# Fewer TensorE instructions for q and z, and other partitions for the gathered rows

## The chip, the cores and the metric

The kernel runs on one core of one Trainium2 chip. Its time is the device time of one execution in microseconds (us); lower is better. The core has TensorE (matmuls, "PE" in the profile, its weight loads "PEld"), VectorE ("DVE"), ScalarE ("ACT"), GpSimd ("POOL"), SyncE ("SP"), whose queue issues nearly all loads here, and 16 DMA engines that move the bytes.

## What is computed

One token of a decoder layer goes through an attention over a cache and through a gated MLP, and both results are added to the input. Cut to what matters, with D = 576, 32 query heads and 16 key heads of 128, a window W of 4096 positions, and F = 4608, Fh = 2304:

```python
xn = layernorm(x)
q = (xn @ wq).reshape(32, 128)
k, v = last W positions of the caches, each key head for two query heads
o = softmax(q @ k.T * 128 ** -0.5) @ v
z = gelu(xn @ w_in)                       # 4608 values
z1, z2 = z[:Fh], layernorm(z[Fh:])
g = w_sp * z2 + b_sp                      # one position: w_sp and b_sp are numbers
out = x + o.reshape(4096) @ wo + (z1 * g) @ w_out
```

All inputs and the output are bf16. The keys and values of the window are 16 MB each; with the four weight matrices about 51 MB have to be read for one token.

## The kernel before, in words

**Loads.** All large loads are issued by SyncE in one order: wq, K0, K1, w_in, K2, V0, K3, V1, V2, V3, then the ends (w_out, wo in five pieces). K and V come in four groups of four heads, each a tile of 128 partitions by 32768 bytes. There are four large buffers (a, b, c, d); a load waits until the work that reads its buffer's last content is done (lines 105 to 120).

**w_out and its gathered rows.** Row f of w_out belongs to partition f // 18, place f % 18. Of the 18 rows of a partition, 15 (NM) come with the load at line 117. The last three (NX) of each partition are 3456 bytes in one piece, and come through two indirect loads that GpSimd issues (load_ext, line 303), each for 128 partitions with an index for each of them. In the first, the partitions in SPARED have the index FAR, which is out of bounds, so nothing is moved for them. In the second, the partitions in GIVEN take the rows of the spared partitions, and all others are FAR. So 32 partitions' rows are loaded to other partitions. The matching values of the MLP are moved to the same partitions by a matmul with the 0/1 matrix `move` (line 546), into hx. The indices are built on GpSimd as a diagonal matrix (`both`, lines 269 to 284), turned into a column on TensorE (`pick`, lines 286 to 288) and cast by VectorE after the first key transposes (rows_to_take, line 290).

**q.** 36 matmuls make q in PSUM (qps), spread over partitions 0, 1, 32, 33, and so on (line 236). It is copied four times into q_rep, two copies by VectorE, two by ScalarE (lines 243 to 247), so that 16 matmuls can turn it into columns that stand in all four blocks of 32 partitions (line 253). Sixteen VectorE operations then write Qb, the weights for the scores, each with a mask (mask4) that leaves one block and zeros the rest (line 264).

**Attention.** For each group and each half of the window, VectorE transposes the keys in blocks of 32 (keys, line 321), and TensorE makes the scores with Qb (line 328). Softmax (sm_a, sm_b) and the products with V (pv, line 401) follow group by group; each group's result ends in Y (y_copy, line 434).

**z.** For each of 9 slices of w_in, z_mms runs eight matmuls of 288 columns: two halves of 9 places (ZT), each for four blocks of partitions (line 443). z_exp turns both halves with two transposes of VectorE (line 451), takes the two useful columns and starts the gelu.

**The order** of everything on each engine is written out by hand at the end (from line 501), and each engine runs its instructions in that order. The last piece is a row of matmuls with one column of weights each (out_mms, line 560): 15 places of hv with w_out, 32 of Y with wo, and the gathered rows with hv and hx.

Of the kernel before, what the change touches and what calls it, by code (L numbers as in the profile page):

```python
# [8 lines left out]
FP32 = mybir.dt.float32  # L9
BF16 = mybir.dt.bfloat16  # L10
# [3 lines left out]
AXX = mybir.AxisListType.X  # L14
# [3 lines left out]
HKV = 16  # L18
# [9 lines left out]
NR = 98  # L28
NF = FH // 128
# [3 lines left out]
NM = NF - NX  # L33
PAIRS = NF // NX
FAR = 4096
SPARED = ((20, 8), (52, 8), (84, 6), (90, 2), (116, 4), (120, 4))
GIVEN = (60, 68, 76, 0, 92, 8)
EPS = 1e-5
SCALE = DH ** -0.5
GELU_C = 0.7978845608028654  # L40
NS = 9
ZT = NF // 2


@with_exitstack
def kernel(
# [14 lines left out]
    nc = tc.nc  # L61
    P = nc.NUM_PARTITIONS
# [4 lines left out]
    const = ctx.enter_context(tc.tile_pool(name="const", bufs=1))  # L67
# [5 lines left out]
    more = ctx.enter_context(tc.tile_pool(name="more", bufs=1))  # L73
    ps_s = ctx.enter_context(tc.tile_pool(name="ps_s", bufs=1, space=bass.MemoryType.PSUM))
    ps_o = ctx.enter_context(tc.tile_pool(name="ps_o", bufs=1, space=bass.MemoryType.PSUM))
    ps_m = ctx.enter_context(tc.tile_pool(name="ps_m", bufs=1, space=bass.MemoryType.PSUM))
    ps_a = ctx.enter_context(tc.tile_pool(name="ps_a", bufs=1, space=bass.MemoryType.PSUM))
    ps_b = ctx.enter_context(tc.tile_pool(name="ps_b", bufs=1, space=bass.MemoryType.PSUM))
# [52 lines left out]
    ident = const.tile([P, P], BF16, name="ident")  # L131
    make_identity(nc, ident[:])
    ones_f = const.tile([P, P], FP32, name="ones_f")
# [10 lines left out]
    nc.vector.memset(qps[:], 0.0)  # L144
    mask = const.tile([P, 2], FP32, name="mask")
    nc.vector.reduce_sum(mask[:], ident[:].rearrange("p (r h) -> p h r", h=2), axis=AXX)
    mask4 = const.tile([P, 4], FP32, name="mask4")
    nc.vector.reduce_sum(mask4[:], ident[:].rearrange("p (a x) -> p a x", a=4), axis=AXX)

    cm = const.tile([P, 2, 2], FP32, name="cm")  # L150
    idc = ident[:].rearrange("p (q u y e) -> p u q y e", q=4, u=2, e=2)
    for e in range(2):
# [5 lines left out]
                            axis=mybir.AxisListType.XY)  # L158
# [17 lines left out]
    for n in range(2):  # L176
        t = ps_s.tile([P, 2, 512], FP32, name=f"S{n}")
# [17 lines left out]
    for j in range(NS):  # L195
        nc.tensor.matmul(ps_x[:, j:j + 1], lhsT=xtw[:, j].rearrange("p m h -> p (m h)"), rhs=ones_b[:, 0:1],  # L196
                         start=True, stop=True)
# [28 lines left out]
    move = more.tile([P, P], BF16, name="move")  # L226
    nc.vector.memset(move[:], 0.0)
    XZ = more.tile([P, NS, 32], BF16, name="XZ")
# [5 lines left out]
    for s, wv in wq_sb:  # L234
        for g in range(4):
            nc.tensor.matmul(  # L236
                qps[32 * g:32 * g + 2, :], lhsT=XT[:, s, :], rhs=wv[:, 512 * g:512 * (g + 1)],
                start=(s == 0), stop=(s == NS - 1), tile_position=(0, 32 * g),
            )

    q_rep = const.tile([P, 8, 2, 4, 32], BF16, name="q_rep")
    qsv = qps[:].rearrange("p (m d e) -> p m e d", e=2, d=32)
    for a in range(4):
        if a % 2:
            nc.scalar.copy(q_rep[:, :, :, a, :], qsv)  # L245
        else:
            nc.vector.tensor_copy(q_rep[:, :, :, a, :], qsv)  # L247

    qps2 = ps_m.tile([P, 4, 4, 8], FP32, name="qps2", tag="m")
    idq = ident[:].rearrange("p (g x) -> p x g", g=4)[0:NR, 0:2, :]  # L250
    for k in range(4):
        for be in range(4):
            nc.tensor.matmul(
                qps2[:, k, be, :].rearrange("p (r g) -> p r g", r=2),
                lhsT=q_rep[0:NR, 2 * k + be // 2, be % 2].rearrange("p a d -> p (a d)"),
                rhs=idq, start=True, stop=True)

    Qb = const.tile([P, HKV, 4, 4, 2], BF16, name="Qb")
    qbv = Qb[:].rearrange("p (m k) b a h -> p a h k b m", k=2)
    qpv = qps2[:].rearrange("p (k h) b m -> p h k b m", h=2)  # L260
    for a in range(4):
        for h in range(2):
            for k2 in range(2):
                nc.vector.tensor_scalar_mul(qbv[:, a, h, k2], qpv[:, h, k2], mask4[:, a:a + 1])


    for (lo, n), at in zip(SPARED, GIVEN):
        nc.gpsimd.tensor_copy(move[:, at:at + n], ident[:, lo:lo + n])
    both = single.tile([P, 4, P], FP32, name="both", tag="pt")
    which = []  # L270
    for g in range(2):
        col = both[:, 2 * g].bitcast(I32)
        if g == 0:
            nc.gpsimd.iota(col, pattern=[[PAIRS, P]], base=PAIRS - 1, channel_multiplier=0)
            for lo, n in SPARED:
                nc.gpsimd.memset(col[:, lo:lo + n], FAR)
        else:
            nc.gpsimd.memset(col, FAR)
            for (lo, n), at in zip(SPARED, GIVEN):
                nc.gpsimd.iota(col[:, at:at + n], pattern=[[PAIRS, n]], base=PAIRS * lo + PAIRS - 1, channel_multiplier=0)  # L280
        diag = both[:, 2 * g + 1]
        nc.gpsimd.tensor_copy(diag, col)
        nc.gpsimd.tensor_tensor(out=diag, in0=diag, in1=ident[:], op=ALU.mult)
        which.append(diag)

    pick = ps_m.tile([P, 2], FP32, name="pick", tag="m")
    for g, diag in enumerate(which):
        nc.tensor.matmul(pick[:, g:g + 1], lhsT=diag, rhs=ones_f[:, 0:1], start=True, stop=True)

    def rows_to_take():  # L290
        idx = more.tile([P, 2], I32, name="idx")
        nc.vector.tensor_copy(idx[:], pick[:])
        which[:] = [idx[:, g:g + 1] for g in range(2)]

    ext = [ext0[:]]

    def fill_ext():
# [17 lines left out]
    def keys(g, c):  # L315

        kT = ktpool.tile([P, TC, 2, 8, GK, 2], BF16, name=f"kT{g}_{c}", tag="kT")
        src = K[g][:, TC * c:TC * (c + 1), :].rearrange("p t d -> p (t d)").bitcast(FP32)
        dst = kT[:].rearrange("p t b r x e -> p (t b r x e)").bitcast(FP32)
        for n in range(4):  # L320
            nc.vector.transpose(dst[:, 1024 * n:1024 * (n + 1)], src[:, 1024 * n:1024 * (n + 1)])  # L321
        KT[g, c] = kT

    def scores(g, c):
        kv = KT.pop((g, c))[:].rearrange("p (t s) b r x e -> p b e x t r s", s=2)
        for be in range(4):
            for x in range(GK):
                nc.tensor.matmul(  # L328
                    S[g % 2][32 * x:32 * x + 8, c, :],
                    lhsT=Qb[:, GK * g + x, be].rearrange("p a h -> p (a h)"),  # L330
                    rhs=kv[:, be // 2, be % 2, x],
                    start=(be == 0), stop=(be == 3), tile_position=(0, 32 * x),
                )
# [13 lines left out]
    def sm_a(g):  # L347
        s = S[g % 2]
        nc.vector.tensor_reduce(out=mx[:, 0:1], in_=s[:], op=ALU.max, axis=mybir.AxisListType.XY)  # L349
        bk = spread(mx, mb, g, ALU.max, "m")  # L350
        nm = work.tile([P, 1], FP32, name=f"nm{g}", tag="nm")
        nc.vector.tensor_scalar_mul(nm[:], bk[:, 0:1], -SCALE)  # L352
        for x in range(GK):
            lo, hi = 32 * x, 32 * x + 32
            nc.scalar.activation(pz[lo:hi, :, :, x, :], s[lo:hi].rearrange("p a (t r e) -> p (a t) r e", r=8, e=2),  # L355
                                 ACT.Exp, bias=nm[lo:hi, 0:1], scale=SCALE, accum_out=lx[lo:hi, g:g + 1])
        st[g] = {}
# [77 lines left out]


    def z_mms():
        zps = [pool.tile([P, ZT, 32], FP32, name=f"zps{n}", tag="ab"[n]) for n, pool in enumerate((ps_a, ps_b))]
        for s, wv in win_sb:
            wt = wv.rearrange("k (q p t) -> k q t p", q=4, t=NF)  # L440
            for n in range(2):
                for q in range(4):
                    nc.tensor.matmul(zps[n][32 * q:32 * q + 32], lhsT=XZ[:, s, :], rhs=wt[:, q, ZT * n:ZT * (n + 1), :],  # L443
                                     start=(s == 0), stop=(s == NS - 1), tile_position=(0, 32 * q))
        return zps

    def z_exp(zps):
        z = const.tile([P, 2, NF], FP32, name="z")
        zt = q_rep[:].rearrange("p m b a d -> p (m b a d)").bitcast(FP32)[:, 0:32 * NF]
        for n in range(2):  # L450
            nc.vector.transpose(zt[:, 32 * ZT * n:32 * ZT * (n + 1)], zps[n][:].rearrange("p t c -> p (t c)"))  # L451
        nc.vector.tensor_copy(z[:], zt.rearrange("p (t c) -> p t c", c=32)[:, :, 0:2].rearrange("p t h -> p h t"))
        u = const.tile([P, 2, NF], FP32, name="u")
        nc.vector.tensor_mul(u[:], z[:], z[:])
        nc.vector.tensor_scalar(out=u[:], in0=u[:], scalar1=0.044715, scalar2=1.0,
                                op0=ALU.mult, op1=ALU.add)
        nc.vector.tensor_mul(u[:], u[:], z[:])
        th = const.tile([P, 2, NF], FP32, name="th")
        nc.scalar.activation(th[:], u[:], ACT.Exp, scale=-2.0 * GELU_C)
        return z, th  # L460
# [40 lines left out]
    for g in range(2):  # L501
        for c in range(2):
            keys(g, c)
            if g == 0 and c == 0:
                rows_to_take()
            scores(g, c)
            if g == 1 and c == 0:
                sm_a(0)
    zps = z_mms()
# [9 lines left out]
    for n, pool in enumerate((ps_a, ps_b)):  # L519
        t = pool.tile([P, 512], FP32, name=f"acc{n}", tag="ab"[n])  # L520
        acc.append(t[32 * n:32 * n + 1, 0:CUT[n + 1] - CUT[n]])
        nc.tensor.matmul(acc[n], lhsT=ones_b[:, 0:1], rhs=xrow[:, CUT[n]:CUT[n + 1]],
                         start=True, stop=False, tile_position=(0, 32 * n))
# [91 lines left out]
```

## Time and profile before

| | us |
|---|---|
| median of 3 runs (126.38 to 126.44) | 126.39 |
| the profiled execution | 126.42 |
| its span, as the profile shows it | 124.4 |
| PE busy, PEld busy | 71.3, 24.4 |
| DVE busy, ACT busy, POOL busy | 82.1, 42.4, 12.7 |

The span begins with the first instruction of the kernel in the trace and ends with the last. The profile gives the busy time of each engine, the share of time in which the DMA engines were busy (in tenths, for 40 equal slices of the span), and groups of instructions by their line: count, busy time, mean time of one in ns, and idle time of the engine just before them with what ended it. A queue q1 carries the loads of SyncE, q0 the indirect loads, q8 and q14 fetches of instructions. A row of the table of windows has the window, its length, and for each engine its busy time and its number of instructions (x), then TensorE's granted clock, the share of DMA time and the GB/s.

### The profile page before, as it was taken

Reading aid. Unit: us, or ns where it says so; the run is one execution under the profiler, and the core shown is the slowest. Engines: PE = TensorE matmul, PEld = TensorE weight load, DVE = VectorE, ACT = ScalarE, POOL = GpSimd, SP = SyncE. Lnnn points to the kernel's source line nnn. Section 1 sums busy time; section 2 is a strip of 40 time slices with the busy share of each in tenths; the row PEclk is TensorE's granted clock in tenths of the full one; section 3 lists DMA queues with packets and bytes.
Section 4 is the critical chain, followed back from the end, with each engine's and each line's share of the span. In section 5 each row is a group of like instructions: output and inputs, shape, how many; then the busy total and the mean of one; then the engine's idle time right before and its main releaser. Section 6 shows DMA issues by size and latency. Waiting matters only on the chain.

```text
span 124.4 us, 1498 instructions
## 1 busy us (share of the span) xinstructions
PE 71.3 (57%) x547; PEld 24.4 (20%) x547; DVE 82.1 (66%) x166; ACT 42.4 (34%) x94; POOL 12.7 (10%) x45
## 2 busy tenths in 40 slices
PE   0012851308885739999290596109998450499961
PEld 0011201301100001443010012101312210246750
DVE  6745525899699976607999718799992628916001
ACT  2100011000000783999049203921990492700001
POOL 2961730000000000000000000000000170000000
PEclk9999998555996877999959599655699955558998
DMA  4999897999989898999989899999989999999980
GB/s 105 509 424 433 383 506 337 506 424 411 480 358 487 356 516 358 495 411 432 485 369 479 358 495 400 445 463 390 474 369 490 390 453 390 413 440 413 422 340 0
DMA packets 2770, 51.04 MB, mean 410 GB/s; under 512 B 395, under 2 KB 524, under 8 KB 844
## 3 DMA queue, kind: packets, MB, share of 16 engines
q1 hardware_dynamic: 2592, 50.51, 95.0%
q0 software_dynamic: 160, 0.44, 0.9%
q8 instruction: 4, 0.07, 0.2%
q14 instruction: 2, 0.02, 0.0%
q10 hardware_dynamic: 12, 0.00, 0.0%
HBM read 51.40 MB, written 0.00 MB: 413 GB/s over the span
## 4 chain that ended last, share of the span: by engine, by line
DMA 60%; DVE 25%; PE 10%; SPq 2%; issue 1%; ACT 0%; DVEq 0%
DMA k<-in_A_k_cache_dram 37%; DMA end<-in_A_wo_dram 23%; DVE kT L321 18%; PE S L328 7%; DVE pt L366 2%; PE ops L401 2%; SPq L93 2%; PE acc L560 1%; DVE mx L349 1%; DVE on L420 1%; DVE om L411 1%; DVE q_rep L451 1%; PE yps L427 0%; PE lps L384 0%; ACT res L583 0%
## 5 line engine op out<-in xcount | busy, mean ns | idle before, releaser
L328 PE MATMUL S<-kT,Qb 128*8 128x512 bf16 x128 | 32.9, 1160 | 20.7 <-DVE kT L321 20.5
L321 DVE STREAM_TRANSPOSE kT<-k 128x1024 f32<-128x1024 f32 x32 | 36.8, 1207 | 6.2 <-DMA k<-in_A_k_cache_dram 6.2
L355 ACT ACTIVATE pz<-S,nm 32x1024 bf16<-32x1024 f32 x16 | 19.1, 1194 | 33.8 <-DVE nm L352 21.2
L372 ACT COPY PT<-pt 32x128 f32<-32x128 f32 x48 | 14.9, 311 | 12.2 <-DVE pt L366 11.7
L328 PEld LDWEIGHTS <-Qb 128*8 128x8 bf16 x128 | 3.5, 97 | 43.5 <-issue 35.1
L366 DVE STREAM_TRANSPOSE pt<-pz 128x1024 f32<-128x1024 f32 x8 | 9.4, 1211 | 3.6 <-ACT pz L355 3.6
L401 PE MATMUL ops<-v,PT 128*32 128x512 bf16 x128 | 10.4, 480 | 1.9 <-ACT PT L377 1.9
L484 POOL TENSOR_TENSOR mz<-mz,mhalf 128x1 f32<-128x1 f32 x1 | 0.6, 566 | 81.9 <-DVE mz L483 81.9
L349 DVE TENSOR_REDUCE mx<-S 128x1 f32<-128x1024 f32 x4 | 4.9, 1215 | 4.6 <-PE S L328 4.6
L443 PE MATMUL zps<-win,XZ 128*32 128x288 bf16 x56 | 7.6, 697 | 0.0
L245 ACT CAST q_rep<-qps 128x512 bf16<-128x512 f32 x2 | 1.2, 585 | 15.0 <-DVE q_rep L247 15.0
L384 PE MATMUL lps<-lx,lsum 128*128 128x1 f32 x8 | 1.9, 304 | 6.5 <-DVE hx L548 4.4
L560 PE MATMUL acc<-end,Y 128*1 128x264 bf16 (+1 forms) x64 | 4.8, 285 | 1.3 <-DMA end<-in_A_wo_dram 1.3
L196 PE MATMUL ps_x<-ones_b,xtw 1*128 1x1 bf16 x9 | 0.4, 163 | 8.9 <-DVE xtw L194 8.9
L443 PEld LDWEIGHTS <-XZ 128*32 128x32 bf16 x72 | 4.2, 117 | 6.2 <-issue 6.2
L583 ACT CAST res<-acc 1x312 bf16<-1x312 f32 x1 | 0.4, 410 | 13.8 <-PE acc L560 13.8
L582 DVE CAST res<-acc 1x264 bf16<-1x264 f32 x1 | 0.4, 421 | 6.9 <-PE acc L560 6.9
L434 DVE CAST Y<-yps 32x32 bf16<-32x32 f32 x4 | 0.7, 187 | 6.4 <-PE yps L427 6.4
L401 PEld LDWEIGHTS <-PT 128*32 128x32 bf16 x128 | 3.6, 113 | 6.0 <-issue 2.3
L420 DVE TENSOR_REDUCE on<-om 128x128 f32<-128x512 f32 x4 | 4.2, 1056 | 0.1
L560 PEld LDWEIGHTS <-Y 128*1 128x1 bf16 x64 | 3.5, 83 | 2.8 <-issue 2.1
L247 DVE CAST q_rep<-qps 128x512 bf16<-128x512 f32 x2 | 1.4, 691 | 3.7 <-PE qps L236 3.1
(116 smaller groups left out, 75.3 us busy)
## 6 DMA issues: line engine op xcount, KB each, us to landing
k<-in_A_k_cache_dram SPq DMA_DIRECT2D x4, 4096.0 KB
v<-in_A_v_cache_dram SPq DMA_DIRECT2D x4, 4096.0 KB, 25.9
win<-in_B_w_in_dram SPq DMA_DIRECT2D x1, 4032.0 KB, 27.2
wq<-in_A_wq_dram SPq DMA_DIRECT2D x1, 3584.0 KB, 12.9
end<-in_B_w_out_dram SPq DMA_DIRECT2D x1, 2160.0 KB, 19.7
end<-in_A_wo_dram SPq DMA_DIRECT2D x1, 2016.0 KB
end<-in_A_wo_dram SPq DMA_DIRECT2D x1, 1296.0 KB
rest<-in_B_w_in_dram SPq DMA_DIRECT2D x1, 1152.0 KB
```

What stands on the lines that cost most here:

```text
L93: nc.sync.dma_start(v, src.rearrange("(p s) c -> p s c", p=P)[:, lo:lo + n, :])
L321: nc.vector.transpose(dst[:, 1024 * n:1024 * (n + 1)], src[:, 1024 * n:1024 * (n + 1)])
L328: nc.tensor.matmul(S[g % 2][32 * x:32 * x + 8, c, :], lhsT=Qb[:, GK * g + x, be].rearrange("p a h -> p (a h)"), rhs=kv[:, be // 2, be % 2, x],
L349: nc.vector.tensor_reduce(out=mx[:, 0:1], in_=s[:], op=ALU.max, axis=mybir.AxisListType.XY)
L355: nc.scalar.activation(pz[lo:hi, :, :, x, :], s[lo:hi].rearrange("p a (t r e) -> p (a t) r e", r=8, e=2), ACT.Exp, bias=nm[lo:hi, 0:1], sc ...
L366: nc.vector.transpose(dst[:, 1024 * n:1024 * (n + 1)], src[:, 1024 * n:1024 * (n + 1)])
L372: nc.scalar.copy(o, i)
L384: nc.tensor.matmul(lps[:, 0:1], lhsT=lsum[:].rearrange("p v y e -> p (v y e)"), rhs=lx[:, g:g + 1], start=True, stop=True)
L401: nc.tensor.matmul(ops[32 * q:32 * q + 32, :], lhsT=d["PT"][:, t0 // 2:t0 // 2 + 2].rearrange("p t x h e -> p (t x h e)"), rhs=V[g][:, t0: ...
L420: nc.vector.reduce_sum(on[:], om[:].rearrange("p c d -> p d c"), axis=AXX)
L443: nc.tensor.matmul(zps[n][32 * q:32 * q + 32], lhsT=XZ[:, s, :], rhs=wt[:, q, ZT * n:ZT * (n + 1), :], start=(s == 0), stop=(s == NS - 1), ...
L560: nc.tensor.matmul(acc[n], lhsT=lhs[:, col:col + 1], rhs=wv[:, CUT[n]:CUT[n + 1]], start=False, stop=last, tile_position=(0, 32 * n))
```

## The change

- **q**: one copy into q_rep, half by VectorE and half by ScalarE; 4 matmuls instead of 16, each for two of the eight pieces (e and d with m). Qb is zeroed once, and 16 copies of 32 partitions each, eight on VectorE and eight on ScalarE, write its blocks from the one turned q; mask4 goes.
- **z**: TZ = 16 of the 18 places are made by four matmuls of 512 columns (one for each block of partitions), the last 2 places of all four blocks by one matmul of 256 columns into partitions 0 to 31. Five matmuls a slice instead of eight. z_exp has one transpose of 512 columns and four of 32 partitions by 64 columns.
- **indices**: pick and its matmuls go; VectorE sums the rows of the diagonal matrices, and rows_to_take runs before the keys instead of after the first of them.
- **SPARED and GIVEN**: 22 partitions are spared instead of 32, and their rows are spread in pairs over partitions that stand a step apart.

The diff, cut to its core:

```diff
-SPARED = ((20, 8), (52, 8), (84, 6), (90, 2), (116, 4), (120, 4))
-GIVEN = (60, 68, 76, 0, 92, 8)
+SPARED = ((20, 4), (52, 4), (84, 8), (116, 4), (120, 2))
+GIVEN = ((24, 4), (40, 8), (64, 4), (112, 12), (0, 4))
...
-ZT = NF // 2
+TZ = 16
...
-    mask4 = const.tile([P, 4], FP32, name="mask4")
-    nc.vector.reduce_sum(mask4[:], ident[:].rearrange("p (a x) -> p a x", a=4), axis=AXX)
+    Qb = const.tile([P, HKV, 4, 4, 2], BF16, name="Qb")
+    nc.vector.memset(Qb[:], 0.0)
...
-    for a in range(4):
-        if a % 2:
-            nc.scalar.copy(q_rep[:, :, :, a, :], qsv)
-        else:
-            nc.vector.tensor_copy(q_rep[:, :, :, a, :], qsv)
+    nc.vector.tensor_copy(q_rep[:, 0, 0:4], qsv[:, 0:4])
+    nc.scalar.copy(q_rep[:, 0, 4:8], qsv[:, 4:8])
...
     for k in range(4):
-        for be in range(4):
-            nc.tensor.matmul(
-                qps2[:, k, be, :].rearrange("p (r g) -> p r g", r=2),
-                lhsT=q_rep[0:NR, 2 * k + be // 2, be % 2].rearrange("p a d -> p (a d)"),
-                rhs=idq, start=True, stop=True)
+        nc.tensor.matmul(
+            qps2[:, k, :].rearrange("p (r g) -> p r g", r=2),
+            lhsT=q_rep[0:NR, 0, 2 * k:2 * k + 2].rearrange("p m e d -> p (m e d)"),
+            rhs=idq, start=True, stop=True)
...
     for a in range(4):
-        for h in range(2):
-            for k2 in range(2):
-                nc.vector.tensor_scalar_mul(qbv[:, a, h, k2], qpv[:, h, k2], mask4[:, a:a + 1])
+        for be in range(4):
+            o, i = qbv[32 * a:32 * a + 32, a, be], qpv[32 * be:32 * be + 32]
+            if be % 2:
+                nc.scalar.copy(o, i)
+            else:
+                nc.vector.tensor_copy(o, i)
...
-    pick = ps_m.tile([P, 2], FP32, name="pick", tag="m")
-    for g, diag in enumerate(which):
-        nc.tensor.matmul(pick[:, g:g + 1], lhsT=diag, rhs=ones_f[:, 0:1], start=True, stop=True)
...
     def rows_to_take():
+        take = more.tile([P, 2], FP32, name="take")
         idx = more.tile([P, 2], I32, name="idx")
-        nc.vector.tensor_copy(idx[:], pick[:])
+        for g, diag in enumerate(which):
+            nc.vector.reduce_sum(take[:, g:g + 1], diag, axis=AXX)
+        nc.vector.tensor_copy(idx[:], take[:])
         which[:] = [idx[:, g:g + 1] for g in range(2)]
 
+    rows_to_take()
...
-            for n in range(2):
-                for q in range(4):
-                    nc.tensor.matmul(zps[n][32 * q:32 * q + 32], lhsT=XZ[:, s, :], rhs=wt[:, q, ZT * n:ZT * (n + 1), :],
-                                     start=(s == 0), stop=(s == NS - 1), tile_position=(0, 32 * q))
+            for q in range(4):
+                nc.tensor.matmul(zps[0][32 * q:32 * q + 32], lhsT=XZ[:, s, :], rhs=wt[:, q, 0:TZ, :],
+                                 start=(s == 0), stop=(s == NS - 1), tile_position=(0, 32 * q))
+            nc.tensor.matmul(zps[1][0:32], lhsT=XZ[:, s, :], rhs=wt[:, :, TZ:NF, :],
+                             start=(s == 0), stop=(s == NS - 1), tile_position=(0, 0))
...
-        for n in range(2):
-            nc.vector.transpose(zt[:, 32 * ZT * n:32 * ZT * (n + 1)], zps[n][:].rearrange("p t c -> p (t c)"))
+        nc.vector.transpose(zt[:, 0:32 * TZ], zps[0][:].rearrange("p t c -> p (t c)"))
+        for q in range(4):
+            nc.vector.transpose(zt[32 * q:32 * q + 32, 32 * TZ:32 * NF], zps[1][0:32, q].rearrange("p t c -> p (t c)"))
...
             keys(g, c)
-            if g == 0 and c == 0:
-                rows_to_take()
             scores(g, c)
```

In GIVEN, each entry is now a first partition and a step: the n spared partitions of the SPARED entry beside it go, two by two, to the pair at the first partition, the pair a step further, and so on. The loops that fill `move` and the indices use it through a small function, `given`.

More of the change, by code (lines that the diff above doesn't have):

```diff
@@ L239 @@
             )
-    q_rep = const.tile([P, 8, 2, 4, 32], BF16, name="q_rep")
+    q_rep = const.tile([P, 4, 8, 2, 32], BF16, name="q_rep")
     qsv = qps[:].rearrange("p (m d e) -> p m e d", e=2, d=32)
-    for a in range(4):
-        if a % 2:
-            nc.scalar.copy(q_rep[:, :, :, a, :], qsv)
-        else:
-            nc.vector.tensor_copy(q_rep[:, :, :, a, :], qsv)
-    qps2 = ps_m.tile([P, 4, 4, 8], FP32, name="qps2", tag="m")
+    nc.vector.tensor_copy(q_rep[:, 0, 0:4], qsv[:, 0:4])
+    nc.scalar.copy(q_rep[:, 0, 4:8], qsv[:, 4:8])
@@ L250 @@
+    qps2 = ps_m.tile([P, 4, 8], FP32, name="qps2", tag="m")
     idq = ident[:].rearrange("p (g x) -> p x g", g=4)[0:NR, 0:2, :]
     for k in range(4):
-        for be in range(4):
-            nc.tensor.matmul(
-                qps2[:, k, be, :].rearrange("p (r g) -> p r g", r=2),
-                lhsT=q_rep[0:NR, 2 * k + be // 2, be % 2].rearrange("p a d -> p (a d)"),
-                rhs=idq, start=True, stop=True)
-    Qb = const.tile([P, HKV, 4, 4, 2], BF16, name="Qb")
-    qbv = Qb[:].rearrange("p (m k) b a h -> p a h k b m", k=2)
@@ L260 @@
-    qpv = qps2[:].rearrange("p (k h) b m -> p h k b m", h=2)
-    for a in range(4):
-        for h in range(2):
-            for k2 in range(2):
-                nc.vector.tensor_scalar_mul(qbv[:, a, h, k2], qpv[:, h, k2], mask4[:, a:a + 1])
-    for (lo, n), at in zip(SPARED, GIVEN):
-        nc.gpsimd.tensor_copy(move[:, at:at + n], ident[:, lo:lo + n])
+        nc.tensor.matmul(
+            qps2[:, k, :].rearrange("p (r g) -> p r g", r=2),
+            lhsT=q_rep[0:NR, 0, 2 * k:2 * k + 2].rearrange("p m e d -> p (m e d)"),
+            rhs=idq, start=True, stop=True)
@@ new lines, with given @@
+    qbv = Qb[:].rearrange("p (m k) b a h -> p a b m k h", k=2)
+    qpv = qps2[:].rearrange("p (k h) m -> p m k h", h=2)
+    for a in range(4):
+        for be in range(4):
+            o, i = qbv[32 * a:32 * a + 32, a, be], qpv[32 * be:32 * be + 32]
[3 more added lines that the diff above has]
+                nc.vector.tensor_copy(o, i)
+    def given(t, n, at, step):
+        return t.rearrange("p (k e) -> p k e", e=2)[:, at // 2:(at + step * (n // 2 - 1)) // 2 + 1:step // 2, :]
@@ L269 @@
+    for (lo, n), (at, step) in zip(SPARED, GIVEN):
+        nc.gpsimd.tensor_copy(given(move[:], n, at, step), ident[:, lo:lo + n].rearrange("p (k e) -> p k e", e=2))
     both = single.tile([P, 4, P], FP32, name="both", tag="pt")
@@ L278 @@
             nc.gpsimd.memset(col, FAR)
-            for (lo, n), at in zip(SPARED, GIVEN):
-                nc.gpsimd.iota(col[:, at:at + n], pattern=[[PAIRS, n]], base=PAIRS * lo + PAIRS - 1, channel_multiplier=0)
+            for (lo, n), (at, step) in zip(SPARED, GIVEN):
+                nc.gpsimd.iota(given(col, n, at, step), pattern=[[2 * PAIRS, n // 2], [PAIRS, 2]],
+                               base=PAIRS * lo + PAIRS - 1, channel_multiplier=0)
         diag = both[:, 2 * g + 1]
@@ L437, in z_mms @@
     def z_mms():
-        zps = [pool.tile([P, ZT, 32], FP32, name=f"zps{n}", tag="ab"[n]) for n, pool in enumerate((ps_a, ps_b))]
+        zps = [ps_a.tile([P, TZ, 32], FP32, name="zps0", tag="a"),
+               ps_b.tile([P, 4, NF - TZ, 32], FP32, name="zps1", tag="b")]
         for s, wv in win_sb:
             wt = wv.rearrange("k (q p t) -> k q t p", q=4, t=NF)
-            for n in range(2):
-                for q in range(4):
-                    nc.tensor.matmul(zps[n][32 * q:32 * q + 32], lhsT=XZ[:, s, :], rhs=wt[:, q, ZT * n:ZT * (n + 1), :],
-                                     start=(s == 0), stop=(s == NS - 1), tile_position=(0, 32 * q))
+            for q in range(4):
[3 more added lines that the diff above has]
+                             start=(s == 0), stop=(s == NS - 1), tile_position=(0, 0))
         return zps
@@ L448, in z_exp @@
         z = const.tile([P, 2, NF], FP32, name="z")
-        zt = q_rep[:].rearrange("p m b a d -> p (m b a d)").bitcast(FP32)[:, 0:32 * NF]
-        for n in range(2):
-            nc.vector.transpose(zt[:, 32 * ZT * n:32 * ZT * (n + 1)], zps[n][:].rearrange("p t c -> p (t c)"))
+        zt = q_rep[:].rearrange("p a m b d -> p (a m b d)").bitcast(FP32)[:, 0:32 * NF]
+        nc.vector.transpose(zt[:, 0:32 * TZ], zps[0][:].rearrange("p t c -> p (t c)"))
+        for q in range(4):
+            nc.vector.transpose(zt[32 * q:32 * q + 32, 32 * TZ:32 * NF], zps[1][0:32, q].rearrange("p t c -> p (t c)"))
         nc.vector.tensor_copy(z[:], zt.rearrange("p (t c) -> p t c", c=32)[:, :, 0:2].rearrange("p t h -> p h t"))
```

## The prediction

> **What bounds the kernel now.** I read the share of DMA time over the span first, then the chain that ended last, then the waits of the load queue, then the tail. From the page:
>
> ```profile
> DMA  4999897999989898999989899999989999999980
> ...
> q1 hardware_dynamic: 2592, 50.51, 95.0%
> q0 software_dynamic: 160, 0.44, 0.9%
> q8 instruction: 4, 0.07, 0.2%
> ...
> DMA 60%; DVE 25%; PE 10%; SPq 2%; issue 1%; ACT 0%; DVEq 0%
> ```
>
> From 3 us to 121 us the 16 DMA engines are hardly ever free. Beside the loads there are 160 packets of the indirect gather and four instruction fetches of 16 KB (0.07 MB in 4 packets). The end of the timeline:
>
> ```profile
> 117.92 0.30 PE L560 MATMUL acc<-ext,hx 128*1 128x312 bf16 x1
> 118.47 1.36 PE L560 MATMUL acc<-end,Y 128*1 128x264 bf16 x18 [0.26 <-DMA end<-in_A_wo_dram]
> ...
> 120.54 1.38 PE L560 MATMUL acc<-end,Y 128*1 128x264 bf16 x18 [0.70 <-DMA end<-in_A_wo_dram]
> ```
>
> TensorE stands idle 0.26 us and 0.70 us for the last pieces of wo, so what ends the kernel is the slowest DMA engine's last packet, and nothing that computes. After that packet comes a fixed tail.
>
> The trace also keeps each DMA packet's start, length, size and queue, which no view prints. I put the packets in 16 rows, one for each engine, by letting each start where another ended. In every row the packets follow each other without a gap from 2 us on. The rows end between 120.67 and 121.23 us, 120.94 on average. The last is 121.23; the span ends 3.17 us later at 124.40, and the execution's time is 126.42, 2.02 above the span. The median of the runs is 126.39, 0.03 lower. So the sum is: the latest engine's end, plus 3.17, plus 2.02.
>
> **What lies on an engine's row.** The loads are the same for all. What differs:
> - Gather packets of 6912 bytes (two partitions each) take 0.262 us, a skipped pair 0.009 us. One packet more or less is 0.253 us.
> - Four rows have no valid gather packet at all. Each of them carries one 16 KB fetch (36.6, 65.6, 94.8, 117.8 us). A fetch pushes its row back by 1.42 us (loads that take 9.68 us on other rows take 11.10 there); being spared four packets gives back 1.01.
> - Seven rows have two packets over their four, two have one, three none. Two of those three carry an 8 KB fetch of another sequencer, at 25.5 and 80.1 us, which costs 0.83 and 0.56 us. The first of them is the row that ends last.
>
> One map of partitions to engines fits these counts to SPARED and GIVEN: blocks of four partitions go round eight engines, 0 to 7 for the lower 64 partitions, 8 to 15 for the upper. The spared ones are then 5, 6, 13, 14; those with none given are 1, 3, 4. The Trainium skill, "DMA: Bandwidth & Descriptors", The descriptor swizzle, gives the same map as a formula, so trace and page agree.
>
> **The TensorE stream.** Matmuls and loads begun by each 16 KB fetch, from the busy time in five windows, cut at the fetches:
>
> ```profile
> 0.00:36.64 36.64, 14.55 (x100) 4.39 (x101) 24.91 (x64) 2.45 (x3) 9.88 (x42) 0.86 0.98 413
> 36.64:65.57 28.93, 22.08 (x124) 5.52 (x120) 21.80 (x33) 17.09 (x38) 0.00 (x0) 0.82 0.98 421
> 65.57:94.75 29.18, 17.64 (x126) 4.29 (x126) 22.92 (x35) 15.04 (x37) 0.00 (x0) 0.77 1.02 438
> 94.75:117.84 23.09, 13.91 (x168) 8.33 (x165) 12.04 (x35) 7.42 (x16) 2.83 (x3) 0.70 0.99 422
> ```
>
> That is 201, 445, 697 and 1030 of 1094. 16 KB is 256 instructions if one has 64 bytes; steps of 256, 512, 768, 1024 fit when the sequencer is 55 to 71 ahead of a waiting array at the first three, and level with it at the fourth, where the array runs fast. The diff takes away 12 matmuls for q, 27 for z, and pick's 2 (x4 in the trace, being fp32): 43 and as many weight loads, 86; the change's own count is 79. The stream then ends at 1008 to 1015, plus about 12 semaphore and end instructions. So it ends within 3 beyond and 16 short of the fourth step: I take it that the fetch at 117.8 goes, with little margin.
>
> The Trainium skill, "Runtime: NRT & Kernel Launch", Instruction fetch mechanics, also has refills of 16 KiB for 256 instructions, and calls the cost of crossing a block mostly hidden. By that rule a fetch less is worth nothing. It is hidden from TensorE here, but not from the engine that carries it (1.42 us).
>
> **Engine by engine after.** SPARED is now 11 pairs: 5 and 13 lose four, 14 loses three. GIVEN puts one each on 0, 2, 4, 6, 7, 8, 9, 10, 11, 12, 15.
> - 2, 7, 8, 9, 10, 11, 15: from two to one, so at most 121.13 - 0.25 = 120.88.
> - 0, 12: unchanged, about 120.70.
> - 6, taken as the carrier of the fourth fetch: 120.93 - 1.42 + 5 x 0.253 = 120.78.
> - 5, 13, 14: the rows with the three earlier fetches end at 120.75, 120.93 and 121.10; one of them, 14, gets 0.25 more: 121.00, 121.18 or 121.35.
> - 4: one of three rows without an extra: 120.70, 120.96 or 121.23, plus 0.25. I take 120.95, the row without a fetch.
> - The other two of those stay. The row at 121.23 has the 25.5 us fetch, which comes later (VectorE runs about six instructions fewer before it). At a cost of 0.56 to 0.83 it ends at 120.96 to 121.23; I take the middle, 121.10.
>
> All engine time together falls by 1.42, on average 0.09 an engine. The latest is then between 121.10 and 121.49; I take **121.13**, because several rows are at about 121.1. That is 0.10 less than before: 126.32 on the profile's footing, **126.3** on the runs'.
>
> **What lies beside it**, and what it costs if its cover goes:
>
> ```profile
> L443 PE MATMUL zps<-win,XZ 128*32 128x288 bf16 x56 | 7.6, 697 | 0.0
> L451 DVE STREAM_TRANSPOSE q_rep<-zps 128x288 f32<-128x288 f32 x2 | 0.8, 439 | 0.0
> L264 DVE TENSOR_SCALAR Qb<-qps,mask 128x32 bf16<-128x32 f32 x16 | 2.7, 349 | 1.3 <-PE qps L253 1.3
> L288 PE MATMUL pick<-ones_f,both 128*128 128x1 f32 x4 | 1.0, 350 | 2.9 <-DVE Qb L264 2.9
> ```
>
> - q, Qb and the index: two casts of 0.69 and two of 0.58 in turn become two half ones side by side; 16 matmuls become 4; 16 Qb operations become 8 on VectorE and 8 on ScalarE; pick becomes two reductions of 128x128 on VectorE (0.27 at 128x128 bf16, L157), which now wait for GpSimd's table (done at 16.84, well before). Some 2 us earlier in all, worth nothing: the first key transposes wait for K0 until 23.74. If it took 1 us more instead, K2's issue (32.96) would move, and its engines are busy with win until 45.
> - z: four matmuls of 512 columns and one of 256 for eight of 288. Four of 288 start every 0.52 us; by columns that is 0.92, and 0.12 to 0.46 for the lone one: 1.04 to 1.38 against 1.03, +0.1 to +3.1 us over nine slices. I take +1. Behind it stand K3's issue at 59.27 (its engines come free from 64.36, an issue needs 1.0: 4.1 us of room) and scores at 61.52, which wait for VectorE.
> - z's transposes: 0.80 us becomes one of 512 columns (0.44 at 288, 1.21 at 1024: 0.67) and four of 32 partitions (0.21 at 32 columns, 0.24 apart), 1.6: **+0.8 us** on VectorE, bounds 0.4 to 2.2. VectorE's chain carries that to Y of the last group (114.82). TensorE has 0.34 + 0.26 + 0.70 = 1.30 us of idle before its last stretch, so it is covered.
> - Gather indices: POOL issues the gather at 99.61 from an index that was ready at 28.4; it is ready earlier now.
> - Tail: same instructions. The granted clock is 1.00 from 113.1 to 123.35.
>
> **Rivals.**
> 1. The fetch stays (the change does not do what it says): the fourth step lies inside the stream. The sequencer reaches it while TensorE waits at 118 to 120.5, and engine 6, no longer spared, keeps its 120.93 and gets five packets, 1.27: 122.20, or 127.4, **slower**. It decides from about 12 instructions more than I count. For it: the thin margin. Against: the change takes away just enough. 0.12.
> 2. The rows come out more even, with late rows starting earlier and the 8 KB fetch at 0.56: the latest at about 120.9, 126.42 - 0.33 = 126.1, **faster**. Against: the row with the 36.6 us fetch ends at 121.10 already. 0.15.
> 3. Bad luck in the map: engine 4 is a row with a fetch, or 14 is the late one: 121.35 to 121.49, 126.5 to 126.7. 0.07.
> 4. VectorE's +0.8 is 2.2: 0.9 beyond the cover, 127.3. 0.04.
>
> **How the numbers follow.** My forecast, 126.3, within 126.14 to 126.64: 0.62. A difference of 0.2% (0.25 us) is about what a measurement of this kernel can tell. Faster: rival 2, 0.15. Slower: rivals 1, 3 and 4, 0.23. The range, 126.05 to 126.7, takes in 2 and 3 and leaves out 1 and 4 (0.16).
>
> **What would show it.** Three 16 KB fetches on queue 8 instead of four; 64 gather packets still; rows that end between 120.7 and 121.2; last matmuls that begin for the DMA as now. A fourth fetch, or idle that VectorE ends before the last 18 matmuls, would make it wrong.

## The result and the profile after

The changed kernel takes **127.38 us** (median of 21 runs, 126.64 to 127.99), the kernel before 126.41 in the same session (126.34 to 126.65): a ratio of 1.0068, interval 1.005 to 1.0087. It is 0.97 us slower, outside the predicted range, and its runs are spread over 1.35 us where those of before lie within 0.31. The profiled execution took 127.14 with a span of 124.86, which is 2.28 between them instead of 2.02.

From the page of the changed kernel, the lines that answer to those of before:

```profile
DMA  4999998999989898998989999998999989999970
...
q1 hardware_dynamic: 2592, 50.51, 94.7%
q0 software_dynamic: 160, 0.44, 0.9%
q8 instruction: 4, 0.07, 0.2%
...
DMA 60%; DVE 31%; PE 5%; SPq 1%; issue 1%; ACT 0%; DVEq 0%
```

In tenths, the DMA engines are as full as before, and q8 still has **four** fetches of 16 KB. The end of the timeline, as in the prediction:

```profile
118.91 1.36 PE L563 MATMUL acc<-end,Y 128*1 128x264 bf16 x18 [0.28 <-DMA end<-in_A_wo_dram]
...
120.97 1.37 PE L563 MATMUL acc<-end,Y 128*1 128x264 bf16 x18 [0.70 <-DMA end<-in_A_wo_dram]
```

TensorE still waits for the DMA ahead of its last two stretches (0.28 and 0.70 us, before 0.26 and 0.70), so the end is still the latest DMA engine's. The stretches themselves are 0.43 to 0.44 us later: the loads are late, not the arithmetic.

What made them late shows in z. The groups of the changed kernel for z (busy time and mean ns of one after the first bar):

```profile
L445 PE MATMUL zps<-win,XZ 128*32 128x512 bf16 x28 | 9.0, 1085 | 0.0
...
L447 PE MATMUL zps<-win,XZ 128*32 128x256 bf16 x7 | 4.5, 641 | 0.0
...
L456 DVE STREAM_TRANSPOSE q_rep<-zps 32x64 f32<-32x64 f32 x4 | 0.9, 230 | 0.0
...
L454 DVE STREAM_TRANSPOSE q_rep<-zps 128x512 f32<-128x512 f32 x1 | 0.7, 673 | 0.0
```

and its timeline at the end of z:

```profile
58.09 0.64 PE L447 MATMUL zps<-win,XZ 128*32 128x256 bf16 x1
...
59.46 0.64 PE L447 MATMUL zps<-rest,XZ 128*32 128x256 bf16 x1
...
60.83 0.64 PE L447 MATMUL zps<-rest,XZ 128*32 128x256 bf16 x1
...
61.49 0.53 SPq L99 DMA_DIRECT2D k<-in_A_k_cache_dram  x1
```

A slice takes 1.37 us (from one L447 row to the next), where eight matmuls of 288 columns took 1.03. The last two slices read `rest`, the buffer that K3 is to fill, so K3's load is issued when z ends: at 61.49. The same row of the kernel before is

```profile
59.27 0.54 SPq L99 DMA_DIRECT2D k<-in_A_k_cache_dram  x1
```

In the waits of SyncE's queue it is one row of the kernel before,

```profile
SPq L99 <- PE zps L443: 12.1, 1, 12.1
```

which has become, in the changed kernel,

```profile
SPq L99 <- PE zps L447: 14.3, 1, 14.3
```

The trace's packets show what that does. The engines finish V0, the load ahead of K3, from 64.24 on. Before, every engine went on to K3 without a gap, and its first packet took 1.21 us. After, one engine that was done at 64.28 got its first packet of K3 at 65.01, 0.73 later, and needed 0.39 more for the load; it is the last of all at the end (121.65). Four others had first packets of 1.29 to 1.50 us.

### The profile page after: what moved, and what is told of

Its sections match the earlier page's. It is cut to its first block, busy times and chain, and to the rows that moved or that the text cites. A ratio compares the mean times of both kernels' runs of the same rounds, so it can differ in the third digit from the quotient of the medians.

```text
span 124.9 us, 1410 instructions
## 1 busy us (share of the span) xinstructions
PE 72.9 (58%) x504; PEld 20.7 (17%) x504; DVE 81.3 (65%) x162; ACT 42.9 (34%) x101; POOL 12.5 (10%) x42
## 4 chain that ended last, share of the span: by engine, by line
DMA 60%; DVE 31%; PE 5%; SPq 1%; issue 1%; ACT 0%; DVEq 0%
DMA k<-in_A_k_cache_dram 37%; DMA end<-in_A_wo_dram 23%; DVE kT L323 22%; DVE pt L368 4%; PE S L330 3%; SPq L93 1%; PE acc L563 1%; DVE mx L351 1%; DVE on L422 1%; DVE q_rep L456 1%; DVE om L413 1%; DVE q_rep L454 0%; PE yps L429 0%; ACT res L586 0%; DVE rs L394 0%
## 5 line engine op out<-in xcount | busy, mean ns | idle before, releaser
L403 PE MATMUL ops<-v,PT 128*32 128x512 bf16 x128 | 11.0, 504 | 1.9 <-ACT PT L379 1.9
L445 PE MATMUL zps<-win,XZ 128*32 128x512 bf16 x28 | 9.0, 1085 | 0.0
L447 PE MATMUL zps<-win,XZ 128*32 128x256 bf16 x7 | 4.5, 641 | 0.0
L445 PE MATMUL zps<-rest,XZ 128*32 128x512 bf16 x8 | 3.7, 1076 | 0.0
```

What stands on the lines that cost most here:

```text
L403: nc.tensor.matmul(ops[32 * q:32 * q + 32, :], lhsT=d["PT"][:, t0 // 2:t0 // 2 + 2].rearrange("p t x h e -> p (t x h e)"), rhs=V[g][:, t0: ...
L445: nc.tensor.matmul(zps[0][32 * q:32 * q + 32], lhsT=XZ[:, s, :], rhs=wt[:, q, 0:TZ, :], start=(s == 0), stop=(s == NS - 1), tile_position= ...
L447: nc.tensor.matmul(zps[1][0:32], lhsT=XZ[:, s, :], rhs=wt[:, :, TZ:NF, :], start=(s == 0), stop=(s == NS - 1), tile_position=(0, 0))
```

## The experiments

Each experiment was run beside the kernel before (medians of 126.31 to 126.35), and the ratio and its interval go by these runs. "Lead" is the time from K3's issue to 64.2, when the first engine comes free. Theory A: K3 is issued too late. Theory B: the fourth fetch stays, and costs because it meets an engine that is no longer spared. Theory C came up on the way.

### e1: the slices of K3's buffer first

```diff
-        for s, wv in win_sb:
+        for i, (s, wv) in enumerate(win_sb[7:] + win_sb[:7]):
...  (start and stop go by i)
```

> The changed kernel, with one thing different: z takes the two slices of w_in that lie in K3's buffer first, so that buffer is free some 10 us before z ends. Theory A (z ends 2.2 us later, so the load of K3 is issued later than the DMA engines need it, and they stand idle): K3 is issued near 51 instead of 61.5, no packet of K3 starts late, and the time is back to about 126.4, with the spread of the runs down from 1.3 to about 0.3. Theory B (the fourth instruction fetch of TensorE is still there and its engine is no longer spared): no change, about 127.4 and as wide a spread.

Measured: **126.62** (126.48 to 126.72), 1.0021 [1.0013, 1.003]. From the timeline of e1's load queue:

```profile
44.95 0.54 SPq L99 DMA_DIRECT2D v<-in_A_v_cache_dram  x1
51.77 0.53 SPq L99 DMA_DIRECT2D k<-in_A_k_cache_dram  x1
61.38 0.53 SPq L99 DMA_DIRECT2D v<-in_A_v_cache_dram  x1
```

K3 is issued 9.7 us earlier, while z ends as late as in the changed kernel (V1, at 61.38, waits for it). About three quarters of the loss and nearly all of the spread go: A holds, and the end of z by itself costs nothing. 0.29 is left.

### e2 to e4: one part alone, one part undone

e2 is the kernel before with the new z only; e3 the changed kernel with the z of before; e4 the changed kernel with SPARED and GIVEN of before.

```diff
+ZT = NF // 2
...  (e3: z_mms and z_exp as before the change; e2: the kernel before, with those two of the change)
-SPARED = ((20, 4), (52, 4), (84, 8), (116, 4), (120, 2))
-GIVEN = ((24, 4), (40, 8), (64, 4), (112, 12), (0, 4))
+SPARED = ((20, 8), (52, 8), (84, 6), (90, 2), (116, 4), (120, 4))
+GIVEN = ((60, 2), (68, 2), (76, 2), (0, 2), (92, 2), (8, 2))
...  (e4: these alone)
```

> The kernel before with the changed z alone (five matmuls a slice, five transposes); q, pick, SPARED and GIVEN as before. Theory A: K3 is issued near 62, time 127.0 to 127.8 with a wide spread. Theory B: 54 TensorE instructions fewer and all four engines still spared, so 126.4 or less.

> The changed kernel with z as before (eight matmuls a slice). Theory A: K3 is issued near 59 as before, time about 126.4 or up to 0.2 less. Theory B: 54 instructions more than in the changed kernel, so the fourth fetch comes earlier, near 119, and falls wholly on an engine that is not spared: 127 or more.

> The changed kernel with SPARED and GIVEN of before. Theory A: no change, about 127.4, since K3 is as late. Theory B: the engine of the fourth fetch is spared again, so about 126.4.

Measured: e2 **127.81** (127.05 to 128.91), 1.0118 [1.0077, 1.0159], K3 issued at 62.28; e4 **127.53** (126.97 to 127.63), 1.0085 [1.0067, 1.0103], K3 at 61.40. Both are late and widely spread: z alone is enough for A, and the new partitions are not needed for it. e3 has K3 in time (58.27), no long packets, and yet takes **127.56** (127.5 to 127.61), 1.0096 [1.0081, 1.0111]. Its last stretch on TensorE:

```profile
121.48 1.37 PE L561 MATMUL acc<-end,Y 128*1 128x264 bf16 x18 [1.72 <-DMA end<-in_A_wo_dram]
```

TensorE waits 1.72 us, not 0.70: the fourth fetch began at 118.93, its engine ended at 122.06, and all others by 121.06. So B is real too, in e3. In the changed kernel and in e1 the fetch begins at 120.6 to 120.7, when the engines are almost done.

### e5: e1 with the old partitions

The edits of e1 and of e4 together.

> The changed kernel with the slices of w_in that lie in K3's buffer taken first (as in e1) and with SPARED and GIVEN as before the change. Theory A (all that was lost is K3's late issue; the new partitions are harmless): as e1, 126.6 to 126.7, K3 issued at 51.8, no long packets at 64 to 65. Theory B (the fourth 16 KB fetch falls on an engine that is no longer spared): the fetch at 120.5 to 120.7 now meets a row that ends its loads near 119.6, so nothing waits for it: 126.1 to 126.4, latest row at or below 121.0. Theory C (the new partitions lengthen the execution by 0.2 to 0.3 us outside the span, as in the three profiles that have them): 0.2 to 0.3 less than e1, 126.3 to 126.4, with time minus span 1.98.

Measured: **126.45** (126.23 to 126.88), 1.0014 [1.0003, 1.0026]. Time minus span is 2.01 on average (1.98 in the profiled execution) where e1 has 2.22: theory C. The fourth fetch came at 119.76, earlier than expected, and the latest row ends at 121.16, no earlier than e1's 121.13, so B's gain did not come.

### e6: the slices of K3's buffer seventh and eighth

```diff
+        for i, (s, wv) in enumerate(win_sb[:6] + win_sb[7:] + win_sb[6:7]):
```

> The changed kernel with the two slices of K3's buffer as seventh and eighth of nine, so that K3 is issued one slice of z, 1.375 us, earlier: at 60.1, 4.1 us before the first engine comes free (64.2). If an issue needs 3 to 4 us before it feeds an engine: as e1, 126.5 to 126.75, no packets over 1.3 us near 64. If it needs more than 4.1 us: part of the loss stays, 126.8 to 127.3, with long packets near 64. If K3's issue was not the cause and only the order of the slices mattered in e1: 127.4.

Measured: **126.61** (126.48 to 126.81), 1.0022 [1.0013, 1.0032], as e1. From its load queue:

```profile
60.11 0.54 SPq L99 DMA_DIRECT2D k<-in_A_k_cache_dram  x1
```

All first packets of K3 take 1.21 us and follow V0 without a gap. One slice of z, 1.37 us, removes the whole of loss A: a lead of 4.1 us is enough.

### e7: the kernel before with K3's slices first

The edit of e1, on the kernel before:

```diff
-        for s, wv in win_sb:
+        for i, (s, wv) in enumerate(win_sb[7:] + win_sb[:7]):
```

> The kernel before with the two slices of K3's buffer first: K3 issued at about 51.3 instead of 59.3. Theory A with a needed lead below 5 us: nothing changes, 126.3 to 126.5. If 59.3 was already late for some engines, or if an earlier issue is itself worth something: 125.9 to 126.2.

Measured: **126.29** (126.21 to 126.33), 0.9999 [0.999, 1.0008]. K3 at 51.67 gains nothing over 59.27; the order of the slices is harmless.

### e8: e3 with the old partitions

The edits of e3 and of e4 together, so that of the change only q, Qb and the index are left.

> The kernel before with the new q, Qb and index alone (z, SPARED and GIVEN as before; that is e3 with the old partitions). K3 issued at 58.3, in time. Theory B: the fetch at 118.9 falls on an engine that is spared four packets, so its row ends near 120.9 and not at 122.06: 126.2 to 126.5, 1.0 to 1.3 less than e3. If the loss of e3 came from q, Qb or the index: 127.3 to 127.6 again. Theory C: time minus span 1.98 and not 2.23.

Measured: **126.35** (126.21 to 126.84), 1.0004 [0.9995, 1.0013]. q, Qb and the index cost nothing. Its last stretch, against e3's above:

```profile
120.57 1.36 PE L561 MATMUL acc<-end,Y 128*1 128x264 bf16 x18 [0.69 <-DMA end<-in_A_wo_dram]
```

The fetch comes at the same time (118.92), on an engine that is spared four packets. The wait is 0.69 instead of 1.72, and the spans differ by 0.94 on average (125.35 and 124.41): that is B's price. The Trainium skill, "Runtime: NRT & Kernel Launch", Instruction fetch mechanics, calls the crossing of a block mostly hidden; of these two kernels that is true of e8 alone, and only because its engine has the room.

### e9: the same partitions, six entries

```diff
-SPARED = ((20, 4), (52, 4), (84, 8), (116, 4), (120, 2))
-GIVEN = ((24, 4), (40, 8), (64, 4), (112, 12), (0, 4))
+SPARED = ((20, 4), (52, 4), (84, 4), (88, 4), (116, 4), (120, 2))
+GIVEN = ((24, 4), (40, 8), (64, 4), (72, 4), (112, 12), (0, 4))
```

> e1 (the changed kernel with the slices of K3's buffer first), with the third entry of SPARED and GIVEN written as two entries: the same partitions are spared and given, but GpSimd runs three instructions more, 63 in the trace as before the change instead of 60. Time minus span was 2.21 to 2.22 on average in all runs of kernels with the new partitions and 1.96 to 2.01 in those with the old ones. Theory C1 (the 0.24 hangs on GpSimd's instructions, their number or place): time minus span 1.97, time 126.35 to 126.4. Theory C2 (it hangs on which partitions are spared and given): 2.22, time 126.6 as e1.

Measured: **126.37** (126.25 to 126.88), 1.0002 [0.9988, 1.0016]. Time minus span is 2.00 on average, with the same partitions as e1 (2.22): C hangs on GpSimd's instructions. The page counts only those that keep the engine busy, so 63 and 60 stand there as 45 and 42; e9's line, with GpSimd (POOL) last:

```profile
PE 73.0 (59%) x504; PEld 21.4 (17%) x504; DVE 81.3 (65%) x162; ACT 43.0 (35%) x101; POOL 12.7 (10%) x45
```

and that of the changed kernel:

```profile
PE 72.9 (58%) x504; PEld 20.7 (17%) x504; DVE 81.3 (65%) x162; ACT 42.9 (34%) x101; POOL 12.5 (10%) x42
```

### e10 and e11: fewer slices, to find the fourth step

```diff
+        for i, (s, wv) in enumerate(win_sb[7:] + win_sb[:3]):     (e10; stop at i == 4)
+        for i, (s, wv) in enumerate(win_sb[7:] + win_sb[:5]):     (e11; stop at i == 6)
```

> e1 with four of the nine slices of w_in left out of z (its result is not the reference's z): 20 matmuls and 20 weight loads fewer, so 979 TensorE instructions in the trace instead of 1019. Theory B (the change fell short of the fourth step of the instruction stream, by up to 40): three 16 KB fetches; the time falls by 0 to 0.25 only, to 126.35 to 126.6, since in e1 the fetch began at 120.6, when its engine had about 0.4 us of loads left. If the fourth fetch is still there, the step lies over 40 instructions below the end and the prediction's count of steps was wrong altogether: 126.6.

> e1 with two of the nine slices of w_in left out of z (its result is not the reference's z): 999 TensorE instructions in the trace instead of 1019. Theory B with a step less than 20 instructions below the end of the changed stream (the prediction had it within 3 of it): three fetches, and a time as e10. If the step lies 20 to 40 below: four fetches, time as e1, 126.6.

Measured: e10 **126.58** (126.43 to 126.86), 1.0014 [1.0002, 1.0027]; e11 **126.61** (126.4 to 127.21), 1.0019 [1.0004, 1.0035]. e10's page:

```profile
q8 instruction: 3, 0.05, 0.1%
```

and e11's:

```profile
q8 instruction: 4, 0.07, 0.2%
```

The fetch goes between 999 and 979 instructions, 20 to 40 below the changed kernel's 1019. And when it is gone the time is that of e1 (126.58 against 126.62).

### e12 and e13: a pair less for the row that ends last

e1 with one more entry, partitions 4 and 5 (e12) or 12 and 13 (e13) spared, their rows given to 32 and 33.

```diff
+SPARED = ((20, 4), (52, 4), (84, 8), (116, 4), (120, 2), (4, 2))      (e12; e13 has (12, 2))
+GIVEN = ((24, 4), (40, 8), (64, 4), (112, 12), (0, 4), (32, 2))
```

> e1 with one more entry: partitions 4 and 5 (DMA engine 1 by the map) are spared as well and their rows go to partitions 32 and 33 (engine 0). Six entries, so GpSimd runs 63 instructions, as in e9. In e7, e9, e10 and e11 the latest or second latest row is the one with the 8 KB fetch at 25.4 or 37.3, an engine with four packets and none given; by the map it is engine 1 or 3. If it is 1: that row has three packets, the latest row ends at 120.9 to 121.0, and the time is 126.1 to 126.3, below before and e9. If it is 3: as e9, 126.35 to 126.4.

> As e12 with partitions 12 and 13 (engine 3 by the map) in place of 4 and 5. If the row with the 8 KB fetch at 37.3 is engine 3: latest row at 120.9 to 121.0, 126.1 to 126.3. If it is engine 1: as e9, 126.35 to 126.4. One of e12 and e13 has to gain; if neither does, the last row is not what ends the kernel.

Measured: e12 **126.45** (126.16 to 126.73), 1.001 [1.0001, 1.0019]; e13 **126.35** (126.24 to 126.95), 1.0008 [0.9998, 1.0019]. In e13 the row with the 8 KB fetch at 37.5 has three packets and ends at about 120.9 in the profile (121.15 in e12), so it is engine 3. The profiled execution of e13 took 126.24, but its median is that of e9 and of before: the gain expected for the right engine did not come. The trace's packets give a reason: in e9's profile the row that ends last is another one, with a single gather packet (by the map engine 14, the only one with one) and the 16 KB fetch at 79.0. It ends at 121.19, and the row with the 8 KB fetch at 120.97. The row of engine 14 is also the last in e12 (121.24) and in e13 (121.05), so a packet less on engine 3 had little to gain. The last row does end the kernel in these profiles: in both, the span ends 3.22 us after the last load, as it does in e9. The rows of the runs that were not profiled are not known.

### e14: the kernel before with three memsets off GpSimd

```diff
-    nc.gpsimd.memset(sel[:], 0.0)
+    nc.vector.memset(sel[:], 0.0)
...  (the same for mx and mb)
```

> The kernel before with three memsets of its start (sel, mx, mb) on VectorE instead of GpSimd: GpSimd runs 60 instructions instead of 63, SPARED and GIVEN as before. Theory C1 as a matter of the number of GpSimd's instructions: time minus span 2.22 instead of 1.97, time 126.55 to 126.6. If the 0.24 belongs to the entries of the new map (their instructions' form or place) and not to the number: 1.97 and 126.3.

Measured: **126.53** (126.46 to 126.64), 1.0015 [1.0007, 1.0024]. Time minus span is 2.21, and the span (124.34 on average) is that of before (124.35). Three GpSimd instructions fewer cost 0.2 us in the kernel before as well:

```profile
PE 70.5 (57%) x547; PEld 24.0 (19%) x547; DVE 82.3 (66%) x169; ACT 42.5 (34%) x94; POOL 12.4 (10%) x42
```

### e15: the lone matmul of one slice last

The changed kernel, with the 256-column matmul of slice 6 issued after the last slice.

```diff
+            if s == 6:
+                w6 = wt
+            else:
                 nc.tensor.matmul(zps[1][0:32], lhsT=XZ[:, s, :], rhs=wt[:, :, TZ:NF, :], ...)
+        nc.tensor.matmul(zps[1][0:32], lhsT=XZ[:, 6, :], rhs=w6[:, :, TZ:NF, :], start=False, stop=True, ...)
```

> The changed kernel with the 256-column matmul of the slice s = 6 moved behind those of the last two slices, so that K3's buffer is free one such matmul earlier, K3 issued at 61.0 instead of 61.5, and z ready as late as in the changed kernel. Theory A with a loss that grows with the lateness, from none at 60.1 to 0.7 at 61.5: 126.8 to 127.2, long packets near 64 but fewer. If the loss is a step that comes with any issue after 60.2: 127.4 as the changed kernel. If the end of z and not K3's issue is what costs: 127.4 too, with K3 in time and no long packets.

Measured: **126.93** (126.59 to 127.4), 1.005 [1.0031, 1.0069]. Its load queue:

```profile
61.11 0.53 SPq L99 DMA_DIRECT2D k<-in_A_k_cache_dram  x1
```

One engine, done at 64.48, got its first packet of K3 0.28 us later, and four first packets took 1.34 to 1.72 us. The loss grows with the lateness among kernels with the same partitions (e6, e15 and the changed kernel; e4 and e2); why e4, with the old ones, loses more than the changed kernel at nearly the same lead is not explained. Mean spans of all runs, each less that of a kernel with K3 in time and the same partitions: 124.38 (e1) for the kernels with the new partitions, 124.48 (e5) for e4, 124.36 (before) for e2:

| kernel | K3 issued | lead | span, mean | lost |
|---|---|---|---|---|
| e1 | 51.77 | 12.4 | 124.38 | 0 |
| e6 | 60.11 | 4.1 | 124.41 | 0.03 |
| e15 | 61.11 | 3.1 | 124.77 | 0.39 |
| e4 | 61.40 | 2.8 | 125.45 | 0.97 |
| changed kernel | 61.49 | 2.7 | 125.09 | 0.71 |
| e2 | 62.28 | 1.9 | 125.85 | 1.49 |

And theory C, time minus span, mean of all runs of each kernel:

| GpSimd instructions | kernels | time minus span |
|---|---|---|
| 63 | before, e2, e4, e5, e7, e8, e9, e12, e13 | 1.95 to 2.01 |
| 60 | changed, e1, e3, e6, e10, e11, e14, e15 | 2.20 to 2.23 |

Of the 0.97 us, then, by these means about 0.7 is K3's late issue and about 0.25 (2.23 less 1.97 of before) lies outside the span; the fourth fetch adds nothing that can be measured. The split is good to about 0.1: the changed kernel and e1 were measured at different times, at which the kernel before took 126.41 and 126.33. e9, which mends both, is level with before. No version beat the kernel before by more than can be measured.

## Why the prediction was wrong, point by point

- **What bounds the kernel**: right. The end is still the slowest DMA engine's: in all 17 profiles the span ends 3.2 to 3.3 us after the last packet of the loads (3.20 before, 3.21 after), so all that moved the span moved that packet.
- **The step that failed**: "K3's issue at 59.27 (its engines come free from 64.36, an issue needs 1.0: 4.1 us of room)". The 1.0 came from the kernel's start, from the first issue at 0.71 to the first packet at 1.71, with idle engines. Between full engines a lead of 4.1 us costs nothing and one of 3.1 costs 0.39 (e6, e15); the need lies between them. Before had a lead of about 5.0, so the room was 0.9 to 1.9 us and not 4.1, and z used 2.2. The prediction named the issue as the thing that stands behind z, but none of its rivals was that this cover runs out. Of the whole 0.97 this step is about 0.7.
- **z's size**: "+0.1 to +3.1 us over nine slices. I take +1". Measured from the first to the last matmul: 9.6 us before (49.6 to 59.2) and 12.5 after (48.9 to 61.5), +2.9; as z began 0.7 earlier, its end moved by 2.2. With +1 and the earlier start its end would have moved by 0.3, which leaves a lead of over 4.1 us, enough by e6: with that size the wrong room would have done no harm. The four of 512 came out as worked out, 0.92; the lone one, which no row of before showed, costs 0.46, the upper of its two bounds, and the value had been taken near the lower.
- **The constant 2.02 around the span**: taken as fixed. It became 2.23, by three GpSimd instructions fewer (e9, e14). No line of the profile of before shows it.
- **The fourth fetch**: "I take it that the fetch at 117.8 goes, with little margin". It stays. The step lies 20 to 40 instructions below the end (e10, e11), where the prediction had the end within 3 beyond and 16 short of it. The inference that the sequencer is level with the array at the fourth fetch does not fit that; how far from it the sequencer is there was not measured.
- **Rival 1**, that the fetch stays: its fact came true, its price did not. It had the fetch at 118 to 120.5 and the engine at 122.20. At 118.9 that is what e3 shows (122.06, a span 0.94 longer than e8's). But in the changed kernel TensorE gets there at 120.7, when the loads are over, and e10 without the fetch is as fast. That the change's time came close to the rival's 127.4 is a coincidence of two other causes.
- **The rows**: the forecast of 121.13 for the latest row is what e1 has (121.13), and with C mended the time is 126.37 (e9) against the predicted 126.3. That it meets to the hundredth is luck: the forecast had three fetches and named no single row, and in e6 and e9 to e13 the last load ends between 121.05 and 121.29, in some on the row with the 8 KB fetch (e6, e11), in others on engine 14's (e9, e10, e12, e13, and e1 too). The map of partitions to engines held: e13's spared pair is taken from the row it names. The row with the 8 KB fetch, taken at 121.10, ends at 120.97 to 121.29 in e6, e9, e10, e11 and e12.
- **q, Qb and the index** at nothing: right (e8, 126.35).
- **z's transposes** at +0.8: 0.67 and 0.92, 1.6 in all against 0.80, and covered as said, since TensorE's last waits are still for the DMA.

## What to carry to other kernels

Where DMA engines never stop, the number to guard for each load is its lead: the time from its issue to the end of the transfer ahead of it; measure what lead is needed in the full stream, not at the quiet start. Where the next load waits for a buffer, the work that reads this buffer should run first (here the order of the nine slices), since that cost nothing (e7) and turns a long stage into cover. And a small difference of time that the span does not show has to be looked for outside it, by comparing time minus span over all runs, before it is put down to the edit that seems nearest.

## What the runs showed of the hardware

- A load that is issued late does not only leave a gap: the packets that it starts with take longer (1.29 to 1.61 us in the changed kernel, up to 2.15 in e2, instead of 1.21), and the time then varies from run to run, by 1.35 us in the changed kernel, 0.66 in e4 and 1.86 in e2. A lead of 3.1 us is already too short for a 4 MB load. What in the queue takes this time was not settled.
- A 16 KB fetch of instructions costs its engine what it delays there, so its price goes from nothing at 120.6 (e1 against e10) to 0.94 us at 118.9 on an engine without room (e3 against e8), by when TensorE gets to that place in its stream.
- Three short GpSimd instructions more or fewer move 0.24 us outside the span, in all the kernels tried. Whether that is in the number, the length or the place of the stream's end is open; only 63 and 60 were tried.
- Some kernels with K3 in time (e5, e8, e9, e10, e11, e12, e13) have single runs 0.3 to 0.6 us above their medians, e1 and e7 have none; the kernel before has them too (126.70 beside e5, 127.14 beside e9). One such run each of e5, e9 and e12 is long outside the span (time minus span 2.36 to 2.48), the others within it. This is not explained.
